# One v load cut in two, q tile 2 prepared earlier, and FFN steps regrouped in the opening of a fused attention and FFN kernel

## The chip, the cores and the metric

The kernel runs on one core of a Trainium2 chip. The metric is the device time of one execution in microseconds (us). The kernel before took 327.85 us (median of 3 runs, 327.48 to 328.96) when the prediction was made.

PE is the matmul engine, PEld its weight loads, DVE the vector engine, ACT the scalar engine, POOL the GpSimd engine, and SP the sync engine, which issues most loads. In the traces q1 is the queue of the loads that SP issues (hardware descriptors), and q0 the queue of the loads that POOL issues (software descriptors).

## The reference, cut to what matters

```python
# batch, heads, tokens, head_dim = 8, 8, 576, 64; d_model 512; d_ff 1536
r = np.maximum(x, 0.0)
phi(x) = np.concatenate([r * cos_w, r * sin_w], axis=-1)   # cos_w, sin_w by token
kv  = einsum('bhsf,bhsd->bhfd', phi(k), v);  z = sum(phi(k), axis=s)
x   = einsum(phi(q), kv) / (einsum(phi(q), z) + 1e-6)      # n/d below
xn  = x / rms(x) * rms_g
out = (silu(xn @ w_gate) * (xn @ w_val)) @ w_out
```

Everything before the FFN is small work for PE. The FFN is most of it: 12 steps of 128 columns for every 512 tokens, then the output matmuls.

## The kernel before

The kernel fills PE with FFN matmuls of one batch while DVE and ACT prepare the attention of the next. Only the opening, batch 0, has nothing to hide behind. It does, in this order: load k, q, v; phi of k; cast v to bf16; kvz, which is phi(k) times v with the sum z; copy kvz out of PSUM; n/d by tiles of 128 tokens; sum of squares (`x_sq`, ACT and POOL); normalize (`x_norm`, DVE); transpose x on PE; evacuate the transpose; FFN. `filler` matmuls keep PE busy meanwhile.

The parts that the change touches (cuts are marked):

```python
    load_kv("k", 0, *LOW); load_kv("k", 0, *HIGH)        # pairs of heads 0-1 and 2-3
    load_q_tokens(0, 0, 2)
    first_v = load_kv("v", 0, *LOW)
    load_kv("v", 0, 2, 3)
    load_kv("v", 0, 3, 4)                                # the last v pair, one DMA
    load_q_tokens(0, 2, 4)
    # ... constants, phi of k, q tiles 0 and 1, first v casts ...
    kvz_mm(0, low_banks, LOW)
    v_cast(V, 0, 3, 4, 0, 5)                             # V: DVE, A: ACT
    v_cast(A, 0, 3, 4, 5, NJ)
    kvz_copy(V, 0, 0, low_banks[0], LOW)
    kvz_copy(V, 0, 1, low_banks[1], LOW)
    kvz_mm(0, high_banks, (2, 3))
    # ... n/d of x tiles 0 and 1, x_sq, fillers, x_norm(0, 0) ...
    x_tr_pe(0, 0, psG[1][:, :])
    x_tr_evac(V, 0, 0, psG[1][:, :])
    q_tr_pe(0, 2, psO[0][:, :])
    q_tr_evac(A, 0, 2, psO[0][:, :])
    # ...
    open_ffn(0, (0,), 0, 128)                            # FFN step 0 for x tile 0
    x_tr_pe(0, 1, psV[1][:, :])
```

The FFN weights are loaded by POOL in ten slices, numbered 0 to 9, two for each range of columns. The load of k of batch 1 waits for slice 7. Its phi is put behind FFN steps 8 to 10, on DVE and ACT, in the same queues as the silu of those steps:

```python
    d = load_kv("k", 1)
    tc.add_manual_dep(d.ins, weight_dmas[7].ins.name, SYNC_DEP, reason="after the weights")
    gate_q = load_q(1)
    load_kv("v", 1, *LOW); load_kv("v", 1, *HIGH)
    # ...
    for j in range(NJ):
        at(0, 8 + j // 4, "post", k_phi, V, 1, j, 0)
        at(0, 8 + j // 4, "post", k_phi, A, 1, j, 1)
    for c in range(2):
        at(0, 10 + c, "post", q_phi, V, 1, c, 0)
        at(0, 10 + c, "post", q_phi, A, 1, c, 1)
    # ... later, among the output matmuls of batch 0: phi of q tiles 2 and 3 of batch 1,
    # then v_cast of batch 1, then kvz_pe(1, psA) ahead of the fourth
```

## Time and profile before

| | before, first profile |
|---|---|
| span | 326.24 us |
| PE busy | 98% of the span |
| first v landing | 10.28 us |
| n/d of the first half of x tile 0 | 12.89 us |
| transposes of x tile 0 | 17.10 us |
| first 128x512 FFN matmul (step 6) | 30.76 us |
| first phi of k of batch 1 on ACT | 35.77 us |
| kvz of batch 1 on PE | 44.70 us |

The page's chain of waits, followed back from the last instruction; the first line is by engine, the second by line of the kernel:

```profile
PE 90%; DMA 2%; DVE 2%; ACT 2%; issue 1%; SPq 0%; POOL 0%; ACTq 0%
PE psG L425 26%; PE psC L445 26%; PE psV L425 26%; PE psA L281 3%; DMA rv<-in_v_dram 2%; PE psA L309 2%; PE psG L445 1%; PE psG L561 1%; PE psO L561 1%; PE psV L561 1%; ACT kpm L208 1%; PE psC L826 1%; PE psV L253 1%; ACT sg L434 0%; PE psA L316 0%
```

Nine tenths of the chain are PE. Loads appear only as the v load at the start. The timeline of PE shows the opening. Its columns are start, duration, engine, line, operation, what is written and read, shapes, count, and in brackets the idle time before and what ended it:

```profile
12.89 0.30 PE L325 MATMUL psV<-kvzs,qpT 128*128 128x65 bf16 x4
...
17.10 0.40 PE L411 MATMUL psG<-ident,xn 128*128 128x128 bf16 x4 [0.89 <-DVE xn L386]
...
18.03 0.39 PE L561 MATMUL psG<-xnT,wg 128*128 128x128 bf16 x4
...
18.68 0.40 PE L411 MATMUL psV<-ident,xn 128*128 128x128 bf16 x4
...
23.68 0.40 PE L411 MATMUL psA<-ident,xn 128*128 128x128 bf16 x4
...
30.76 1.03 PE L425 MATMUL psG<-xnT,wg 128*128 128x512 bf16 x4
...
44.70 1.33 PE L281 MATMUL psA<-vvm,kpm 64*128 64x65 bf16 x72
```

The transposes of x tile 0 wait 0.89 us for the normalized x. From them to the first FFN matmul are 0.93 us, which the evacuation takes. From 30.76 us on, PE shows no idle time worth a mark.

### The profile page before, as it was taken

The page shows a single profiled execution, that of the slowest core. Times are in us where ns is not written, and L with a number is a line of the kernel's source. Part 1 is how long each engine was busy: PE and PEld are TensorE (multiplying, and loading weights), DVE is VectorE, ACT ScalarE, POOL GpSimd, SP SyncE. Part 2 cuts the span into 40 slices and gives each one's busy share as a digit, 9 for nine tenths or more (in the row PEclk, how much of TensorE's full clock was granted, in tenths as well). Part 3 has the DMA queues.
Part 4 walks back from the last instruction along what each step waited for, and adds up shares of the span by engine and source line. Part 5 has one row for each costly group of instructions (what it writes and reads, how often), then busy time and mean ns, then how long its engine had stood idle before and what let it go on. Part 6 is the DMA issues. An engine that isn't in the chain of part 4 may idle for free.

```text
span 326.2 us, 6439 instructions
## 1 busy us (share of the span) xinstructions
PE 318.8 (98%) x2442; PEld 161.0 (49%) x2442; DVE 186.3 (57%) x414; ACT 175.6 (54%) x364; POOL 32.3 (10%) x67
## 2 busy tenths in 40 slices
PE   8989999999999999999999999999999999999995
PEld 2478465554445444544454445444544444444443
DVE  6775668787755766578257745773577133203410
ACT  6774775865666457645655476556644233223321
POOL 1660212001100110010001100110011000000000
PEclk9999999999999999999999999999999999999999
DMA  7999999799969956976597569957621400020014
GB/s 254 247 186 238 353 196 343 276 172 211 264 181 159 236 166 178 204 210 173 170 223 204 156 187 229 188 161 218 123 44 32 131 32 0 27 104 1 0 34 96
DMA packets 80193, 53.91 MB, mean 165 GB/s; under 512 B 51361, under 2 KB 67489, under 8 KB 80162
## 3 DMA queue, kind: packets, MB, share of 16 engines
q1 hardware_dynamic: 73120, 48.64, 57.9%
q0 software_dynamic: 6880, 4.72, 10.0%
q8 instruction: 19, 0.31, 0.4%
q10 hardware_dynamic: 162, 0.13, 0.1%
q14 instruction: 12, 0.10, 0.1%
HBM read 37.75 MB, written 9.44 MB: 145 GB/s over the span
## 4 chain that ended last, share of the span: by engine, by line
PE 90%; DMA 2%; DVE 2%; ACT 2%; issue 1%; SPq 0%; POOL 0%; ACTq 0%
PE psG L425 26%; PE psC L445 26%; PE psV L425 26%; PE psA L281 3%; DMA rv<-in_v_dram 2%; PE psA L309 2%; PE psG L445 1%; PE psG L561 1%; PE psO L561 1%; PE psV L561 1%; ACT kpm L208 1%; PE psC L826 1%; PE psV L253 1%; ACT sg L434 0%; PE psA L316 0%
## 5 line engine op out<-in xcount | busy, mean ns | idle before, releaser
L440 DVE TENSOR_TENSOR hT<-psV,sg 128x512 bf16<-128x512 f32 x102 | 70.3, 689 | 96.6 <-PE psV L425 84.9
L434 ACT ACTIVATE sg<-psG 128x512 f32<-128x512 f32 x102 | 60.5, 594 | 64.9 <-PE psG L425 64.8
L425 PE MATMUL psG<-xnT,wg 128*128 128x512 bf16 (+1 forms) x368 | 92.9, 375 | 0.1
L425 PE MATMUL psV<-xnT,wv 128*128 128x512 bf16 (+1 forms) x368 | 92.7, 374 | 0.0
L445 PE MATMUL psC<-wo,hT 128*128 128x512 bf16 x396 | 89.6, 379 | 0.0
L425 PEld LDWEIGHTS <-wv 128*128 128x128 bf16 x416 | 40.6, 98 | 47.4
L445 PEld LDWEIGHTS <-hT 128*128 128x128 bf16 x420 | 40.2, 98 | 46.4
L425 PEld LDWEIGHTS <-wg 128*128 128x128 bf16 x416 | 38.6, 98 | 41.3 <-DVE xnT L264 0.4
L262 ACT COPY osb<-psC 128x512 f32<-128x512 f32 (+1 forms) x33 | 19.2, 582 | 40.7 <-PE psC L445 39.4
L379 POOL TENSOR_TENSOR rs<-ms,mhalf 128x1 f32<-128x1 f32 x36 | 20.0, 556 | 200.7 <-ACT scr L374 200.7
L374 ACT ACTIVATE scr<-xt 128x513 bf16<-128x513 f32 x36 | 22.9, 635 | 24.0 <-DVE xt L363 22.9
L386 DVE SCALAR_TENSOR_TENSOR xn<-xt,rs,gb 128x512 bf16<-128x512 f32 x36 | 26.8, 745 | 14.7 <-POOL rs L379 14.7
L208 ACT ACTIVATE kpm<-rk,tab 128x256 bf16<-128x256 f32 (+1 forms) x78 | 31.8, 477 | 1.6 <-DMA rk<-in_k_dram 1.6
L363 DVE TENSOR_TENSOR xt<-psA,rec 128x512 f32<-128x512 f32 x35 | 24.2, 691 | 1.2
L210 DVE TENSOR_SCALAR kpm<-rk,tab 128x256 bf16<-128x256 f32 (+1 forms) x84 | 22.1, 329 | 2.1 <-DMA rk<-in_k_dram 2.1
L208 ACT ACTIVATE qp<-rq,tab 128x512 bf16<-128x512 f32 x31 | 21.7, 712 | 0.0
L210 DVE TENSOR_SCALAR qp<-rq,tab 128x512 bf16<-128x512 f32 x33 | 15.5, 484 | 0.2 <-DMA rq<-in_q_dram 0.2
L309 PEld LDWEIGHTS <-qpT 128*128 128x128 bf16 x248 | 11.6, 98 | 6.7 <-issue 0.3
L309 PE MATMUL psA<-kvzs,qpT 128*128 128x65 bf16 x248 | 12.8, 194 | 0.2
L425 PE MATMUL psG<-xnt_tail,wg 128*128 128x512 bf16 x48 | 12.3, 379 | 0.0
L425 PE MATMUL psV<-xnt_tail,wv 128*128 128x512 bf16 x48 | 12.3, 379 | 0.0
L281 PEld LDWEIGHTS <-kpm 64*128 64x128 bf16 x576 | 9.9, 95 | 3.9 <-issue 2.9
(89 smaller groups left out, 168.4 us busy)
## 6 DMA issues: line engine op xcount, KB each, us to landing
out_dram<-osb SPq DMA_DIRECT2D x32, 256.0 KB, 2.9
rv<-in_v_dram SPq DMA_DIRECT2D x22, 288.0 KB, 3.4
rk<-in_k_dram SPq DMA_DIRECT2D x20, 288.0 KB, 3.6
rq<-in_q_dram SPq DMA_DIRECT2D x20, 256.0 KB, 3.2
rk<-in_k_dram SPq DMA_DIRECT2D x2, 1152.0 KB
rq<-in_q_dram SPq DMA_DIRECT2D x2, 1024.0 KB, 10.7
rv<-in_v_dram SPq DMA_DIRECT2D x3, 576.0 KB, 9.7
wo<-in_moe_w_out_dram POOLq DMA_DIRECT2D x4, 384.0 KB, 6.9
```

The lines of the kernel that those rows point to most:

```text
L208: nc.scalar.activation(out=out_ap, in_=in_ap, func=AF.Relu, scale=scale)
L210: eng.tensor_scalar(out=out_ap, in0=in_ap, scalar1=scale, scalar2=0.0, op0=ALU.mult, op1=ALU.max)
L281: nc.tensor.matmul(banks[c][:, r * E : (r + 1) * E], lhsT=kp_main[b][lo : lo + 64, j, r, :], rhs=vvm[b % 2][lo : lo + 64, r, j, :], start= ...
L309: nc.tensor.matmul(o[:, g, i, :], lhsT=qpT[(b, 0)][:, h, j * P : (j + 1) * P], rhs=kvz_of(b, h), start=True, stop=True,)
L363: nc.vector.tensor_tensor(out=xt[:, 0:DM].rearrange("p (b h d) -> p b h d", b=2, d=D), in0=o[:, :, :, 0:D], in1=rec[:, :, :].unsqueeze(3). ...
L374: nc.scalar.activation(out=scr[:, :], in_=xt[:, 0 : DM + 1], func=AF.Square, scale=1.0 / math.sqrt(DM), accum_out=ms[:, :],)
L379: nc.gpsimd.tensor_tensor(out=rs[:, :], in0=ms[:, :], in1=mhalf[:, :], op=ALU.pow)
L386: nc.vector.scalar_tensor_tensor(out=xn[:, :], in0=x_of[(b, j)][:, 0:DM], scalar=rs_of[(b, j)][:, :], in1=gb[:, :], op0=ALU.mult, op1=ALU. ...
L425: nc.tensor.matmul(pst[bank][:, cols[0] : cols[1]], lhsT=w[:, t, n * P : (n + 1) * P], rhs=x[:, t, cols[0] : cols[1]], start=(t == 0), sto ...
L434: nc.scalar.activation(out=sg[:, :], in_=psG[bank][:, :], func=AF.Silu)
L440: nc.vector.tensor_tensor(out=hTs[blk][:, n, :], in0=psV[bank][:, :], in1=sg[:, :], op=ALU.mult)
L445: nc.tensor.matmul(bank, lhsT=hTs[blk][:, n, j * P : (j + 1) * P], rhs=wo[:, n, :], start=(n == 0), stop=(n == NNT - 1),)
```

## The change

The intent was to shorten the opening: let the casts of the last v pair begin when its first piece has landed, free DVE of the low kvz copies, use ACT's and PE's idle time around 14 to 17 us for q tile 2, and give PE two FFN steps wherever it waited for the next x tile. The core of the diff:

```diff
-    def load_kv(which, b, r0=0, r1=4):
+    def load_kv(which, b, r0=0, r1=4, j0=0, j1=NJ):
... (source and target take columns j0 * D to j1 * D)
-    load_kv("v", 0, 3, 4)
+    load_kv("v", 0, 3, 4, 0, 5)
+    load_kv("v", 0, 3, 4, 5, NJ)
...
     kvz_mm(0, low_banks, LOW)
+    kvz_copy(A, 0, 0, low_banks[0], LOW)
+    kvz_copy(A, 0, 1, low_banks[1], LOW)
     v_cast(V, 0, 3, 4, 0, 5)
-    v_cast(A, 0, 3, 4, 5, NJ)
-    kvz_copy(V, 0, 0, low_banks[0], LOW)
-    kvz_copy(V, 0, 1, low_banks[1], LOW)
+    v_cast(V, 0, 3, 4, 5, NJ)
     kvz_mm(0, high_banks, (2, 3))
-    filler(1, idle)
-    kvz_mm(0, high_banks, (3, 4))
-    q_tr_evac(A, 0, 1, psO[0][:, :], (0, 4))
     nd_half(0, 0, 0, psV[0])
     nd_post_half(0, 0, 0, psV[0])
+    q_tr_evac(A, 0, 1, psO[0][:, :], (0, 4))
+    kvz_mm(0, high_banks, (3, 4))
     kvz_copy(A, 0, 0, high_banks[0], HIGH)
     kvz_copy(A, 0, 1, high_banks[1], HIGH)
+    filler(1, idle)
...
+    q_phi(A, 0, 2, 1)
     x_sq(0, 0)
...
+    q_phi(A, 0, 2, 0)
     x_sq(0, 1)
...
-    q_phi(A, 0, 2, 1)
-    filler(9, psV[1][:, :])
+    filler(7, psV[1][:, :])
+    q_tr_pe(0, 2, psO[0][:, :])
     x_norm(0, 0)
-    q_phi(V, 0, 2, 0)
+    q_tr_evac(A, 0, 2, psO[0][:, :])
     q_phi(A, 0, 3, 1)
+    filler(1, psV[1][:, :])
...
     x_tr_evac(V, 0, 0, psG[1][:, :])
-    q_tr_pe(0, 2, psO[0][:, :])
-    q_tr_evac(A, 0, 2, psO[0][:, :])
...
-    open_ffn(0, (0,), 0, 128)
+    open_ffn(0, (0, 1), 0, 128)
     x_tr_pe(0, 1, psV[1][:, :])
     x_tr_evac(V, 0, 1, psV[1][:, :])
-    open_ffn(0, (1,), 0, 128, first=1)
...
-    open_ffn(2, (4,), 0, 256, parts=(0,))
+    open_ffn(2, (4, 5), 0, 256, parts=(0,))
     x_tr_pe(0, 2, psA[:, 0, :])
     x_tr_evac(A, 0, 2, psA[:, 0, :])
-    open_ffn(2, (5,), 0, 256, first=1, parts=(0,))
```

More of the change, by code (lines that the diff above doesn't have):

```diff
@@ L79, in load_kv @@
         return nc.sync.dma_start(
-            out=raw[key][:, r0:r1, :],
+            out=raw[key][:, r0:r1, j0 * D : j1 * D],
             in_=src[b, 2 * r0 : 2 * r1, :, :]
             .rearrange("h s d -> (h s d)")
-            .rearrange("(r p n) -> p r n", p=P, n=NJ * D),
+            .rearrange("(r p n) -> p r n", p=P, n=NJ * D)[:, :, j0 * D : j1 * D],
         )
```

## The prediction

> **What bounds the kernel.** The page gives a span of 326.2 us with PE busy 98%, and the chain of waits puts 90% on PE. From about 31 us on PE runs without a gap over 0.4 us, and none there waits for a DMA (waits of PE and PEld after 30 us). The change touches only the opening, 10 to 25 us, so it can only move when that stream begins.
>
> **The opening, from the timeline and the chain.** DMA gates it until the last v pair lands near 11.8; then kvz of that pair 12.49 to 12.95; second n/d half; its xt on DVE at 14.37; x_sq on ACT 14.89; rs on POOL 15.69; xn on DVE 16.30 to 17.05; x transposes on PE at 17.10. Fillers cover PE to 16.2, then 0.89 us idle. After 17.10 I see three places where PE loses time: 0.7 us from the x transposes to the first FFN matmul (the evacuation; the eight q transposes, 0.44 us, hide inside it), 0.2 us before 18.68 (xn of x tile 1), 0.3 us before 23.68 (xn of x tile 2).
>
> **The change, costed.**
> 1. *v in two pieces, low copies to ACT.* One more issue (0.44 to 0.6 us on a queue that runs 6 us ahead of the data). The runs fall from 2304 to 1280 and 1024 bytes, above the 512 bytes that the Trainium skill ("DMA: Bandwidth & Descriptors", Specifications) gives for line rate; no run here has tested it. DVE now casts both pieces (0.49 and about 0.4 us), so the last kvz stays near 12.5. But ACT copies the low kvz at about 11.85 to 12.3 (DVE: 12.22 to 12.70), so n/d half 0 goes from 12.89 to about 12.35 and its DVE work (0.83 us) ends near 13.5 instead of 14.05. DVE was what held half 1 (PE finished it at 13.73, DVE began it at 13.97). Half 1, x_sq, rs, xn and the x transposes move forward 0.2 us, to about 16.9.
> 2. *q tile 2 ahead.* Phi moves from DVE (0.48) to ACT (0.71) and fits in ACT's idle time around 14 and between the x_sq; q lands at 13.3. Its transposes fill PE's idle time. They were in the shadow of the evacuation: worth about 0.
> 3. *Two FFN steps before x tile 1's transposes.* Removes the 0.2 us wait at 18.68. Gain 0.2.
> 4. *Steps 4 and 5 before x tile 2's transposes.* Removes 0.3 us at 23.68; its evacuation is still covered, by 0.87 us of matmuls, just enough.
>
> Sum about 0.7 us, all on the chain. Weights land at least 1 us before use (wv slice 0 at 17.1 for 18.1), as do q, v and wo of the next batch, so the stream should keep the shift to the end.
>
> **Prediction.** 327.2 us (before: 327.85), 8 in 10 between 326.4 and 328.1. Faster by over 2%: 0.01; within 2%: 0.98; slower by over 2%: 0.01.
>
> **What would show it.** The timeline: n/d half 0 before 12.5; x transposes of tile 0 near 16.9; no gap ahead of tile 1's transposes nor tile 2's; the first 128x512 FFN matmul of step 6 at about 30.1 instead of 30.76; the same distance from there to the end.
>
> **What would make it wrong.** The second v piece landing over 0.3 us later; phi of q tile 2 holding ACT when x_sq could start; the q transposes or the filler behind them holding the x transposes; DMA holding the later stages.

## More of the kernel before

Times are medians of 3 to 11 runs. Each set of runs was made on one chip, the later sets on four different ones, so times are compared only within a set or as ratios to the kernel before. All runs compared here were fast, that is within 1.5% of the fastest of their kernel.

The timeline of ACT around the next batch's k (the last line is the cast of v of batch 1):

```profile
35.28 0.60 ACT L434 ACTIVATE sg<-psG 128x512 f32<-128x512 f32 x1 [1.13 <-PE psG L425]
35.77 1.69 ACT L208 ACTIVATE kpm<-rk,tab 128x256 bf16<-128x256 f32 x4
...
43.25 1.15 ACT L262 CAST vvm<-rv 128x1152 bf16<-128x1152 f32 x1
```

The phi of k begins directly behind the silu of step 8 and shows no wait. From there to the v cast ACT is never idle, and the kvz of batch 1 on PE follows that cast.

## The result

Before 328.25 us (median of 6 runs, 327.48 to 329.6), changed 329.09 us (6 runs, 328.53 to 329.76). The ratio is 1.0023, with a 95% interval of 0.9998 to 1.0048. Ratios here are formed from the fast runs of both kernels in the same rounds, so they are not quite the ratio of the medians quoted. The two lie within 2% of each other, as forecast, but the time is above the forecast range and the forecast gain did not come.

The changed kernel's chain of waits, first profile (span 327.92 us; its line numbers are one higher than before, four higher for the opening's FFN matmuls):

```profile
PE 83%; DMA 8%; ACT 4%; DVE 1%; issue 1%; SPq 1%; POOL 0%; ACTq 0%
PE psC L446 26%; PE psG L426 24%; PE psV L426 24%; DMA rk<-in_k_dram 3%; PE psA L282 3%; DMA wv<-in_moe_w_val_dram 3%; DMA rv<-in_v_dram 2%; PE psA L310 2%; ACT kpm L209 2%; PE psG L446 1%; ACT sg L435 1%; PE psC L826 1%; PE psV L254 1%; ACT qp L209 0%; PE psA L317 0%
```

PE's share fell from 90% to 83%, and two loads are new: a weight slice (wv) and k of batch 1. The timeline of PE, at the same places as before:

```profile
12.74 0.37 PE L326 MATMUL psV<-kvzs,qpT 128*128 128x65 bf16 x4
...
17.47 0.40 PE L412 MATMUL psG<-ident,xn 128*128 128x128 bf16 x4
18.38 0.38 PE L565 MATMUL psG<-xnT,wg 128*128 128x128 bf16 x4 [0.52 <-DVE xnT L265]
...
19.27 0.39 PE L412 MATMUL psV<-ident,xn 128*128 128x128 bf16 x4
...
23.95 0.39 PE L412 MATMUL psA<-ident,xn 128*128 128x128 bf16 x4
...
30.59 1.03 PE L426 MATMUL psG<-xnT,wg 128*128 128x512 bf16 x4
...
39.64 1.02 PE L426 MATMUL psG<-xnT,wg 128*128 128x512 bf16 x4 [0.25 <-ACT sg L435]
...
43.20 0.38 PE L446 MATMUL psG<-wo,hT 128*128 128x512 bf16 x1 [1.03 <-ACT sg L435]
...
46.13 1.33 PE L282 MATMUL psA<-vvm,kpm 64*128 64x65 bf16 x72
```

Measured from the first v landing, which came at 10.84 us in this run and at 10.28 before, the opening became shorter: step 6 starts 19.75 us after it, and 20.48 before. That is the forecast gain, 0.73 us. But then PE waits twice for a silu, at 39.64 and at 43.20, and kvz of batch 1 is 1.43 us later than before instead of earlier. The timeline of ACT shows why:

```profile
35.11 0.60 ACT L435 ACTIVATE sg<-psG 128x512 f32<-128x512 f32 x1 [1.13 <-PE psG L426]
37.40 1.71 ACT L209 ACTIVATE kpm<-rk,tab 128x256 bf16<-128x256 f32 x4 [1.70 <-DMA rk<-in_k_dram]
39.01 0.57 ACT L435 ACTIVATE sg<-psG 128x512 f32<-128x512 f32 x1
...
44.89 1.15 ACT L263 CAST vvm<-rv 128x1152 bf16<-128x1152 f32 x1
```

ACT has done the silu of step 8 at 35.7 us and then stands for 1.70 us until k of batch 1 has landed. The silu of step 9, which PE needs, comes behind the phi of k in ACT's queue. The chain in order of time (start, duration, what), from 17 us on, says the same:

```profile
18.56 8.88 DMA wv<-in_moe_w_val_dram
...
27.46 9.91 DMA rk<-in_k_dram
...
37.40 0.03 ACT kpm L209
...
37.81 1.29 ACT kpm L209 x3
...
43.20 0.38 PE psG L446
...
46.20 1.27 PE psA L282 x72
```

A weight slice issued at 18.56 us lands at 27.4; that releases the load of k, which takes 9.91 us; then ACT works without a pause until its cast of v ends at 46.04, 0.09 us before PE's kvz.

The 1.68 us between the two profiled spans add up from six stretches: the first v landing +0.56, from it to the x transposes -0.19, from them to step 6 -0.54, from step 6 to the first phi of k +1.80, from that to kvz -0.20, and from kvz to the end +0.25.

### The profile page after: what moved, and what is told of

It reads as the page before. It is cut to its first block, busy times and chain, and to the rows that moved or that the text cites. A ratio compares the mean times of both kernels' runs of the same rounds, so it can differ in the third digit from the quotient of the medians.

```text
span 327.9 us, 6438 instructions
## 1 busy us (share of the span) xinstructions
PE 318.9 (97%) x2441; PEld 161.0 (49%) x2441; DVE 185.9 (57%) x412; ACT 176.5 (54%) x366; POOL 32.1 (10%) x67
## 4 chain that ended last, share of the span: by engine, by line
PE 83%; DMA 8%; ACT 4%; DVE 1%; issue 1%; SPq 1%; POOL 0%; ACTq 0%
PE psC L446 26%; PE psG L426 24%; PE psV L426 24%; DMA rk<-in_k_dram 3%; PE psA L282 3%; DMA wv<-in_moe_w_val_dram 3%; DMA rv<-in_v_dram 2%; PE psA L310 2%; ACT kpm L209 2%; PE psG L446 1%; ACT sg L435 1%; PE psC L826 1%; PE psV L254 1%; ACT qp L209 0%; PE psA L317 0%
## 5 line engine op out<-in xcount | busy, mean ns | idle before, releaser
L209 ACT ACTIVATE qp<-rq,tab 128x512 bf16<-128x512 f32 x32 | 22.5, 714 | 0.2 <-DMA rq<-in_q_dram 0.2
```

Source lines behind the costliest of these rows:

```text
L209: nc.scalar.activation(out=out_ap, in_=in_ap, func=AF.Relu, scale=scale)
```

## The experiments

There were two theories at the start. **K**: the gain of the opening is real, but the phi of k of batch 1 can't begin before k lands, and from there on ACT's queue, not PE, decides, so the time is k's landing plus a constant. **S**, the rival: cutting the v load delays the loads of the opening. A second rival, **O**, came with the second set: PE's own work in the opening decides, and k was late by chance in one profile only. Later a third matter, **T**, came up: the longer tail.

Each kernel was profiled once and timed against the kernel before. All the profiles, cut at the same five marks (us; "v" is the first v landing, "x" the transposes of x tile 0, "s6" the first 128x512 matmul, "phi" the first phi of k of batch 1 on ACT, "kvz" the first kvz of batch 1 on PE; the runs in the order of their sections):

| run | v | v to x | x to s6 | s6 to phi | phi to kvz | kvz to end | span |
|---|---|---|---|---|---|---|---|
| before | 10.28 | 6.82 | 13.66 | 5.01 | 8.93 | 281.54 | 326.24 |
| changed | 10.84 | 6.63 | 13.12 | 6.81 | 8.73 | 281.79 | 327.92 |
| before_again | 9.38 | 7.13 | 13.66 | 5.92 | 8.73 | 281.53 | 326.35 |
| after_again | 10.52 | 6.63 | 13.12 | 5.91 | 8.73 | 281.79 | 326.70 |
| no_split | 10.07 | 6.63 | 13.12 | 6.97 | 8.73 | 281.54 | 327.06 |
| after_k5 | 10.04 | 6.70 | 13.12 | 5.01 | 9.17 | 281.77 | 325.81 |
| before_k5 | 10.66 | 7.27 | 13.65 | 5.01 | 8.93 | 281.54 | 327.06 |
| after_k9 | 10.21 | 6.63 | 13.12 | 6.75 | 8.73 | 281.78 | 327.22 |
| before_k9 | 9.97 | 6.82 | 13.66 | 5.95 | 8.73 | 281.52 | 326.65 |
| after_q | 10.24 | 6.64 | 13.12 | 7.20 | 7.80 | 282.23 | 327.23 |
| after_k6 | 10.81 | 7.41 | 13.12 | 5.01 | 8.93 | 281.77 | 327.05 |
| before_k6 | 10.02 | 6.84 | 13.66 | 5.01 | 8.93 | 281.55 | 326.01 |
| part_front | 10.03 | 6.63 | 13.66 | 6.13 | 8.73 | 281.77 | 326.95 |
| part_ffn | 10.50 | 7.65 | 13.30 | 5.48 | 8.73 | 281.54 | 327.20 |
| split_only | 10.02 | 6.84 | 13.66 | 5.83 | 8.73 | 281.76 | 326.84 |
| no_split_k6 | 10.02 | 6.63 | 13.12 | 5.01 | 8.93 | 281.56 | 325.27 |
| no_split_k6_warm | 10.23 | 6.73 | 13.12 | 5.55 | 8.73 | 281.54 | 325.90 |

"x to s6" depends on the order of the FFN, and under the new order also on where the q transposes are (13.30 in part_ffn, 13.12 elsewhere). "s6 to phi" is 5.01 wherever the phi follows the silu of step 8, and more wherever ACT waited for k. "phi to kvz" is 8.73 whenever ACT waited, unless its queue was changed (after_q); kvz then begins 0.09 or 0.10 us after ACT's cast of v ends, and 0.30 us or more after it where ACT did not wait, so it is ACT's queue that PE follows. "kvz to end" has only two values but for after_q. The times:

| run | median us | kernel before, same rounds | ratio | 95% interval |
|---|---|---|---|---|
| after_again | 328.60 | 328.45 | 1.0007 | 0.9986 to 1.0027 |
| before_again | 328.38 | 328.45 | 1.0002 | 0.9988 to 1.0016 |
| no_split | 328.86 | 328.45 | 1.0010 | 0.9996 to 1.0024 |
| after_k5 | 328.08 | 328.45 | 0.9989 | 0.9974 to 1.0004 |
| after_k9 | 329.71 | 328.50 | 1.0035 | 1.0009 to 1.0061 |
| before_k9 | 328.93 | 328.50 | 1.0021 | 0.9997 to 1.0045 |
| before_k5 | 328.86 | 328.50 | 1.0002 | 0.9981 to 1.0023 |
| after_q | 328.31 | 328.50 | 0.9991 | 0.9968 to 1.0014 |
| after_k6 | 328.32 | 328.87 | 0.9991 | 0.9973 to 1.0009 |
| before_k6 | 328.07 | 328.87 | 0.9989 | 0.9969 to 1.0010 |
| part_front | 328.66 | 328.87 | 1.0003 | 0.9983 to 1.0023 |
| part_ffn | 328.87 | 328.87 | 1.0002 | 0.9979 to 1.0025 |
| split_only | 328.44 | 328.84 | 0.9985 | 0.9970 to 1.0001 |
| no_split_k6 | 327.57 | 328.84 | 0.9966 | 0.9949 to 0.9982 |
| no_split_k6_warm | 327.59 | 328.84 | 0.9961 | 0.9949 to 0.9974 |

All of these are within 2%, and most of the intervals include 1. Apart from after_k9 and the last two, the verdicts below therefore rest on the profiles and not on the times.

### after_again and before_again: the two kernels once more

No edit. 

> The changed kernel once more. The question is whether the two profiles differ by the change or by chance. Theory K (the load of k of batch 1 decides): the opening is about 0.7 us shorter in each profile relative to the landing of the first v pair, and the scalar engine's first phi of k of batch 1 starts when that k lands, not when its silu is done; the time is k's landing plus a constant. If the late weights of the first profile (131 KB per us instead of 190 from 13 to 18 us) were chance, k lands near 35.8 here and the span is near 326.2; if the change causes them, k lands at 37 again and the span is near 327.9.

> The kernel before once more, as a measure of chance. Theory K: the phi of k of batch 1 starts at the landing of k or right after the silu of step 8 at 35.8, whichever is later; span 326 to 327.5 with k's landing moving from run to run by up to 1 us. Time ratio to before 1.000 within 0.003.

The changed kernel's opening repeated to 0.01 us. k landed at 36.16, near the earlier of the two values expected, but the phi still waited for it; the span was 326.70, not the 326.2 expected. The kernel before brought the surprise. Its timeline of ACT and its chain:

```profile
34.69 0.60 ACT L434 ACTIVATE sg<-psG 128x512 f32<-128x512 f32 x1 [1.13 <-PE psG L425]
36.09 1.70 ACT L208 ACTIVATE kpm<-rk,tab 128x256 bf16<-128x256 f32 x4 [0.81 <-DMA rk<-in_k_dram]
```

```profile
PE 82%; DMA 7%; DVE 4%; ACT 3%; issue 1%; POOL 0%; ACTq 0%; DVEq 0%
PE psC L445 26%; PE psG L425 24%; PE psV L425 24%; DMA rk<-in_k_dram 4%; DMA wv<-in_moe_w_val_dram 3%; PE psA L281 3%; PE psA L309 2%; ACT kpm L208 2%; PE psG L445 1%; DVE kpm L210 1%; ACT sg L434 1%; PE psC L826 1%; PE psV L253 1%; DVE vvm L264 1%; DVE qp L210 1%
```

In this profile the kernel before waits for k as well: the phi starts 0.81 us late, PE waits 0.56 us for a silu, and k's load and a weight slice are in the chain with PE at 82%. The first profile of before, in which nothing waited, was the lucky one. (Its 7.13 us from v to x is no slow clock: v landed at 9.38 us, and DVE was busy until it could begin the cast at 9.72.) The slow stretch of weights in the first profile of the changed kernel (143 and 91 GB/s in 15:16 and 16:17 us, against 182 and 188 before) also comes without the change: before_again shows 142 and 120 GB/s in 14:15 and 15:16.

### no_split: the changed kernel with one v load

```diff
-    load_kv("v", 0, 3, 4, 0, 5)
-    load_kv("v", 0, 3, 4, 5, NJ)
+    load_kv("v", 0, 3, 4)
```

> The changed kernel with the last v pair loaded in one DMA again. Rival S (the split itself delays the DMA of the opening): v lands at 10.3 instead of 10.84, weights stream at 190 KB per us, k lands near 35.8, time about 1 us under the changed kernel, 327.5 to 328. Theory K without S: landing times and time as the changed kernel within 0.5 us.

v landed at 10.07, but k was no earlier and the time no better (328.86), so S as the cause of the late k falls. The opening is as short without the split (6.63 and 13.12) as with it. The split gains nothing. The first v landing ranges from 9.38 to 10.66 us over the nine profiles without the split and from 10.02 to 10.84 over the eight with it; the ranges overlap, so no delay of the loads is shown. The row holds one more difference: the tail is 281.54 here and 281.79 in the changed kernel.

### after_k5 and before_k5: k of batch 1 issued earlier, in both kernels

```diff
-    tc.add_manual_dep(d.ins, weight_dmas[7].ins.name, ...)
+    tc.add_manual_dep(d.ins, weight_dmas[5].ins.name, ...)
```

> The changed kernel with the load of k of batch 1 gated on weight slice 5 instead of 7, so issued about 4 us earlier. Theory K: k lands before 34.5, the scalar engine no longer waits for it, and the gain of the opening shows: 327.3 to 327.6 us against 328.25 before, 1.5 us under the changed kernel. If the hardware queue's load moves only once the weight queue has drained, k lands no earlier and the time stays near 329.

> The kernel before with k gated on weight slice 5, so early. Theory K: k no longer decides; the start of the step with 128x512 matmuls does, 20.5 us or more after the first v pair landed, and kvz 13.9 to 14.2 us after that. 328.2 to 328.5 us, that is 0.5 to 0.8 us slower than the changed kernel with the same gate was. Rival: no difference from the changed kernel with the early gate, 328.1 or less; then the opening's gain is not worth anything even without the wait.

In the changed kernel k landed at 32.27 us, and ACT no longer waited for it (timeline of ACT):

```profile
34.38 0.60 ACT L435 ACTIVATE sg<-psG 128x512 f32<-128x512 f32 x1 [1.13 <-PE psG L426]
34.87 1.69 ACT L209 ACTIVATE kpm<-rk,tab 128x256 bf16<-128x256 f32 x4
```

Its span, 325.81, is lower than both of the changed kernel's. In time it gained less than expected (328.08, not 327.3 to 327.6). Part of this is that k and the last weight slices are now under way together: slice 9, issued at 19.29, landed at 36.09, where in the changed kernel it was issued at 20.03 and landed at 31.27. The chain in order of time shows that this is just too late for PE:

```profile
19.29 16.79 DMA wv<-in_moe_w_val_dram
36.09 0.05 issue
36.13 1.04 PE psV L426 x4
```

before_k5 also lost its wait for k. Its profile fell into a run with a slow clock (below), so its 7.27 must not be set against 6.63. Its time, 328.86, is above the 328.2 to 328.5 expected; three of its six runs had the low mean clock (0.994) of such a run. The 0.78 us between the medians of the two kernels lie in different rounds on different chips; they go the way that K says, but do not show it.

### after_k9 and before_k9: k of batch 1 issued later, in both kernels

```diff
-    tc.add_manual_dep(d.ins, weight_dmas[7].ins.name, ...)
+    tc.add_manual_dep(d.ins, weight_dmas[9].ins.name, ...)
```

> The changed kernel with the load of k of batch 1 gated on weight slice 9 instead of 7, so later. Theory K (from the landing of that k on, the scalar engine's queue decides, and the PE's first kvz of batch 1 comes 8.7 us after its first phi): first phi near 38.7, kvz near 47.4, span near 329.2, measured time near 331, whatever the opening gained. Rival O (the opening's PE work decides, and k only happened to be late in one profile): time rises by under 0.5 us.

> The kernel before with the same late gate. Theory K: first phi near 38.5, time within 0.4 us of the changed kernel with the late gate, the opening's 0.7 us being invisible. Rival O: 0.7 us slower than the changed kernel with the late gate, or 1 us faster if the change itself costs time.

The size was a miss. k, issued some 4 us later than with slice 7, landed at 36.69 instead of the 38.7 expected. That is 26.48 us after the first v, no later than with slice 7 (26.3 to 27.0 in most profiles), so the spans did not rise. A load issued while weight slices are in flight sent its first packet 3.6 us later, this one, issued behind them, 1.0 us later (last section); and from that packet to its landing it took 4.65 us, where the two profiles of the changed kernel have 6.29 and 5.41. Once more phi to kvz was 8.73 in both, and the opening's difference was gone by the first phi, 26.50 and 26.43 us after v. The medians were 0.8 us apart, not within 0.4 as expected; 0.25 of it is the tail, and the ranges of the two (328.36 to 330.70 and 328.43 to 330.39) cover each other. The ratio of 1.0035 is not told apart from the changed kernel's own 1.0023 (0.9998 to 1.0048).

So this pair, meant to decide between K and O, does not. The earlier gates do. With gate 7 or 9 ACT waited for k in ten of eleven profiles, so k was not late by chance in one; with gate 5 or 6 the wait is gone in five of six, and "s6 to phi" is back at 5.01. O falls. That the gate moves the time is shown by no_split and no_split_k6 (below), which differ by the gate alone: 1.0010 of before (0.9996 to 1.0024) with slice 7, and, in other rounds, 0.9966 (0.9949 to 0.9982) with slice 6.

### after_q: ACT's and DVE's queues relieved behind k

```diff
-        at(0, 10 + c, "post", q_phi, V, 1, c, 0)
-        at(0, 10 + c, "post", q_phi, A, 1, c, 1)
+        at(0, 11, "post", q_phi, V, 1, c, 0)
+        at(0, 11, "post", q_phi, A, 1, c, 1)
... (v_cast of batch 1 ahead of phi of q tiles 2 and 3; q transposes of batch 1 one step later)
```

> The changed kernel with the scalar and vector queues relieved after the landing of k: phi of q of batch 1 moved behind the last silu, the casts of v of batch 1 ahead of half of those phi, the q transposes one step later. Theory K: kvz of batch 1 comes about 7.6 to 8.2 us after the first phi instead of 8.7, the wait of PE for the silu of step 11 shrinks from 0.5 us and over to under 0.2, and the time falls to 327.6 to 328.0. If it stays at 328.6, the scalar queue behind k is not what holds PE.

```profile
37.20 1.70 ACT L209 ACTIVATE kpm<-rk,tab 128x256 bf16<-128x256 f32 x4 [2.08 <-DMA rk<-in_k_dram]
...
43.46 1.15 ACT L263 CAST vvm<-rv 128x1152 bf16<-128x1152 f32 x1
```

The timeline of ACT shows the v cast at 43.46, 6.26 us behind the first phi, where it was 7.49 in the changed kernel. kvz came 7.80 us after the phi instead of 8.73, and 0.39 us after the end of that cast, no longer directly behind it. So it is the queue behind k that lies between k and kvz; the edit relieved ACT and DVE together, and their shares are not separated. PE's wait for the silu of step 11 was 0.42 us, where the changed kernel had 1.03, but not under the 0.2 expected. Half of the gain came back later: the tail was 0.44 us longer than in the changed kernel. I did not follow where. k was 2.08 us late in this profile, and the time (328.31, not the 327.6 to 328.0 expected; ratio 0.9991) is not told apart from before.

### after_k6 and before_k6: the gate between

```diff
-    tc.add_manual_dep(d.ins, weight_dmas[7].ins.name, ...)
+    tc.add_manual_dep(d.ins, weight_dmas[6].ins.name, ...)
```

> The changed kernel with k of batch 1 gated on weight slice 6, between the 5 and the 7 tried. Theory K: k lands near 34 and no longer holds the scalar engine, and the last weight slice lands before 35.5, so PE does not wait for it as it did at 36.09 with gate 5. First phi of k 5.0 us after the first 128x512 matmul, kvz 13.9 us after that matmul; ratio to before 0.997 to 0.999, span near 325.7. If k still lands after 35.5, no gain over gate 7.

> The kernel before with the same gate. Theory K: k was at most just late in it, so ratio to before 0.999 to 1.001, and 0.5 to 0.9 us slower than the changed kernel with gate 6.

With slice 6 neither kernel waits for k or for a weight slice: 5.01 and 8.93 in both rows. before_k6 was a little better than expected (328.07), and the changed kernel was not faster than it in time. Its profile explains part of this: after_k6 ran with a slow clock in the opening and lost 0.78 us there (7.41 instead of 6.63). The runs of both scatter by over 1 us, and this pair alone settles nothing.

The slow clock shows in the stretches view (stretch and its length in us; busy us of PE, PEld, DVE, ACT and POOL with counts; then granted PE clock, DMA share and GB/s). Here 9.0 to 12.5 us of part_ffn, and below it the same of the first profile of before:

```profile
9.00:12.50 3.50, 3.50 (x36) 2.36 (x37) 3.15 (x6) 2.97 (x7) 1.70 (x3) 0.52 0.92 295
```

```profile
9.00:12.50 3.50, 3.21 (x76) 2.11 (x75) 3.09 (x8) 3.00 (x6) 1.92 (x3) 1.00 0.93 285
```

Three of the 17 profiles (before_k5, after_k6, part_ffn) ran at half clock for some 3.4 us here. In the 50 runs of the kernel before in the later sets (before_again's among them), 9 had a mean granted clock of 0.995 or less, about what such a stretch leaves in the mean; they took 329.09 us on average, the other 41 took 328.52. This chance, 0.57 us, is nearly as large as the gain that is being looked for. (Such runs still count as fast.)

### part_front and part_ffn: each half of the change alone

part_front is the changed kernel with the FFN order of before; part_ffn is the kernel before with only the regrouped FFN steps:

```diff
-    open_ffn(0, (0,), 0, 128)
+    open_ffn(0, (0, 1), 0, 128)
     x_tr_pe(0, 1, psV[1][:, :])
     x_tr_evac(V, 0, 1, psV[1][:, :])
-    open_ffn(0, (1,), 0, 128, first=1)
... (the same for steps 4 and 5 around x tile 2)
```

> The changed kernel with the FFN order of before, so only the front: v pieces, copies, phi and transposes of q tile 2. From the first v landing to the x transposes 6.65 us (before 6.8 to 7.3, changed 6.63), from there to the first 128x512 matmul 13.65 as before, not 13.1; time not told apart from before, since k decides.

> The kernel before with only the FFN order of the change. From the first v landing to the x transposes 6.8 to 7.3 us as before, from there to the first 128x512 matmul 13.1 to 13.2 instead of 13.66; time not told apart from before, since k decides.

The front is worth 0.19 us (6.63 against 6.82) and nothing after the x transposes (13.66). (part_ffn's own 7.65 is the slow clock's, above the 6.8 to 7.3 expected.) The FFN order alone is worth 0.36 (13.30), less than expected; with the q transposes out of the way it is worth the whole 0.54 (13.12). In part_ffn the trace has n/d of x tile 2 starting at 20.35 us on PE, released at 20.30 by ACT's evacuation of those q transposes, after 0.16 us in which PE loaded no weights; in the changed kernel it waits for nothing. So the q transposes moved ahead are worth nothing alone and 0.18 us together with the regrouped steps. Which part of the front brings the 0.19 was not separated further; no_split excludes the split of the load, which leaves the copies on ACT and the reordered n/d. In both profiles k decided in the end, and neither time differs from before.

### split_only: the kernel before with the last v pair in two loads

```diff
-    load_kv("v", 0, 3, 4)
+    load_kv("v", 0, 3, 4, 0, 5)
+    load_kv("v", 0, 3, 4, 5, NJ)
```

> The kernel before with only the last v pair in two pieces, its casts as before. Theory T (one more DMA turns the order in which the sync engine checks landings at the end): from the first kvz of batch 1 to the end 281.78 us, as in every kernel with the split, instead of 281.53; the opening as before (first v landing to x transposes 6.8 us or more), k deciding; time 0.0 to 0.5 us over before. Rival: the tail stays 281.53, then the longer tail comes from another part of the change.

The tail was 281.76, so the split alone does it. In all seven profiles with the split and the original later stages it is 281.76 to 281.79 (after_q is left aside), in all nine without it 281.52 to 281.56. The trace shows where. At the end SP waits for the semaphores of the DMAs one after the other, about 0.06 us each. In the kernel before the first such wait ends 280.20 us after kvz, at the landing of SP's last store, and the last store of ACT, which lands at 280.44, is only looked for some waits later. In the changed kernel the first wait ends at 280.45, and seven more follow. The issue view of the last two stores (KB, and us from issue to landing; the landing that the trace lacks is the one with no number), of before and of the changed kernel:

```profile
out_dram<-osb SPq DMA_DIRECT2D x1, 32.0 KB
out_dram<-osb ACTq DMA_DIRECT2D x1, 32.0 KB, 2.0
```

```profile
out_dram<-osb SPq DMA_DIRECT2D x1, 32.0 KB, 1.8
out_dram<-osb ACTq DMA_DIRECT2D x1, 32.0 KB
```

The stores were issued at the same distance from kvz in both (278.39 us). The landing recorded for ACT's store in before, 2.0 us after its issue, fits the first wait's end in the changed kernel. One more DMA at the start turned the order in which the semaphores are used, and the latest one came first. The semaphore numbers in the traces bear this out: the first wait is for number 100 in both, which tells of SP's last store in before and of ACT's in the changed kernel, while ACT's store in before has number 118, the one looked for last. It is so in all 17 profiles: ACT's last store has number 100 in the eight with the split and 118 in the nine without. How the numbers are given out was not looked into; that the split brings the 0.25 us is shown. The time of split_only (0.9985, up to 1.0001) does not show it: 0.25 us is less than the scatter.

### no_split_k6 and no_split_k6_warm: both losses taken away

no_split_k6 is the changed kernel with one load for the last v pair and k of batch 1 gated on slice 6; the second has `filler(2, idle)` in place of `filler(1, idle)` behind each paced matmul of the opening, against the slow clock.

> The changed kernel without the split and with k of batch 1 gated on weight slice 6: both things that hid the opening's gain taken away. Theory K with T: at full clock, first v landing to first 128x512 matmul 19.75, then 13.93 to kvz, then 281.53: span 315.2 us after the first v landing, 325.3 where that lands at 10.1; the kernel before, held by k, has 316.8 (26.5 + 8.73 + 281.53). Ratio to before 0.995 to 0.998. If under 0.1 us faster than before, the accounting is wrong.

> The same with two fillers behind each paced matmul of the opening instead of one. In three of 14 profiles the granted clock of PE halved from about 9.5 to 12.5 us, and the x transposes came 0.5 to 0.8 us later after the first v landing. If idle PE time before that is the reason, no dip here and less scatter: lowest times as without it, highest 0.5 us lower. If the clock dips for another reason, no difference.

The chain of waits and the timeline of ACT of no_split_k6:

```profile
PE 91%; ACT 4%; DVE 2%; issue 1%; DMA 1%; ACTq 0%
PE psC L445 26%; PE psG L425 26%; PE psV L425 26%; PE psA L281 3%; PE psA L309 2%; ACT kpm L208 2%; PE psG L445 2%; PE psG L564 1%; DMA rk<-in_k_dram 1%; PE psV L564 1%; PE psO L564 1%; PE psC L825 1%; PE psV L253 1%; ACT qp L208 1%; ACT sg L434 0%
```

```profile
34.29 0.60 ACT L434 ACTIVATE sg<-psG 128x512 f32<-128x512 f32 x1 [1.13 <-PE psG L425]
34.78 1.69 ACT L208 ACTIVATE kpm<-rk,tab 128x256 bf16<-128x256 f32 x4
```

PE is back at 91% of the chain, and the phi follows the silu. The span is 325.27 with the first v landing at 10.02. That is the best pair, since before_k6 had its v at 10.02 as well, the same full clock in the opening and no wait for k: 326.01. The difference, 0.74 us, is the opening's gain (20.50 - 19.75 = 0.75 us from v to step 6), now whole at the end of the kernel. It is one pair of profiles, from different chips. In time the version takes 0.9966 of before (interval 0.9949 to 0.9982), 1.3 us by the medians. That is below the 2% at which the class changes, but clear of noise, and clear of the changed kernel's ratio (1.0023, from 0.9998), which comes from other rounds. It keeps the change without the split and adds the earlier gate, so not all of it is the change's: before_k6, with the gate alone, has 0.9989 (0.9969 to 1.0010). These intervals overlap, so in time the change's own share is not shown.

The warm version is as fast (0.9961). Neither it nor no_split_k6 had a slow-clock run among six, so whether the extra fillers help is not settled. Its profile had k late by 0.54 us again: gate 6 makes the wait rare, not impossible.

## Why the prediction was wrong, point by point

- *What bounds the kernel: "none there waits for a DMA".* True of the one profile it was read from, not of the kernel. In the second profile of before, PE waits 0.56 us behind ACT, which waits for k. In the first, the phi of k started directly behind a silu with no wait, so k had landed, but nothing in that view says by how much. I took "no wait" for "room". The trace does allow an estimate: q of batch 1, issued right behind k, landed at 38.59 us, and in the five profiles with gate 7 that give both landings q comes 2.9 us (2.89 to 2.95) after k. So k landed near 35.7 in that profile, only some 0.1 us before its phi began at 35.77.
- *Front, gain 0.2.* Right in size: 6.82 to 6.63. The reason given, that DVE was freed early by the copies on ACT, fits, but was not tested apart from the new order of n/d; the v split was not needed for it, as no_split shows. In the changed profile n/d half 0 came 1.90 us after the first v landing instead of 2.61. The Trainium skill ("DMA: Bandwidth & Descriptors", Specifications) asks for 512 bytes or more for line rate, and the pieces of 1280 and 1024 bytes agree with that to within some 0.1 us: with the split the last v landed 1.55 to 1.69 us after the first, without it 1.52 to 1.57.
- *q tile 2, gain 0.* Right alone (part_front 13.66), and it was needed for the next term.
- *FFN order, gain 0.2 + 0.3.* Right: 0.54 for all of it.
- *"Weights land at least 1 us before use [...], as do q, v and wo of the next batch, so the stream should keep the shift to the end."* This is the step that failed. The list leaves out k of batch 1. I had looked at the landings of q, v and wo; for k the trace gave none, and I went on. k needs to land by 5.01 us after step 6 starts, its load is started by the weights and not by PE (slice 7 releases it, and the first slice waits for the first v load), and it lands about 26.5 us after the first v landing whatever PE's opening does (26.3 to 27.0 in nine of the ten profiles in which it decided at gate 7 or 9, 25.66 in after_again, and 25.40 at gate 6 in the warm version). The kernel before wants it 20.48 + 5.01 = 25.49 us after v, the changed one 19.75 + 5.01 = 24.76. So the shorter opening only makes a longer wait for the same load. The first profile of before, which the prediction was read from, escaped by luck: there phi came 25.50 us after v. Term by term: the hand-over from step 6 to phi was put at no change, and was 0.9 and 1.8 us longer than 5.01 in the two profiles of the changed kernel.
- *The tail.* Not foreseen at all: 0.25 us from one more DMA.
- *The time.* Gain 0.73 in the opening, of which nothing reached the end, and 0.25 lost. The measured medians are +0.84 us in the first set and +0.15 in the second, both with intervals that include no change. The sum of the known terms is near +0.25; the rest is not told apart from the scatter of k's landing and of the clock.

Among the dangers that the prediction named, "DMA holding the later stages" was the true one. The slow clock is not among them, and its effect was nearly as large as the gain.

## What to carry to other kernels

Before moving work forward, look for the next load that this work will meet and that does not move along: find its landing, its gate and its first reader, and take a missing landing as an open question. An instruction that starts exactly when its predecessor ends tells nothing about how long its data had been there, so profile twice before calling a stretch free of waits. An in-order queue turns one late load into late work for everyone behind it: here the silu that PE needed stood behind the phi of k.

## What the Trainium skill lacked or had wrong

- "DMA: Bandwidth & Descriptors", Specifications, gives about 0.6 us to the first byte for loads from the sync queue, and its section on queues says that an engine takes turns between the queues that have work. Here, counted from the start of the issuing instruction (which itself takes about 0.5 us), the first packet of q1 came 1.1 us after the first issue of the kernel, but 3.47 to 3.77 us after the issue of k of batch 1 in each of the fifteen profiles with gates 5 to 7, where weight slices of q0 were still outstanding. It came after 1.05 and 1.02 us in the two with gate 9, where all ten slices had landed and q0 had only the end of a load of w_out left. The DMA view of before from 27.5 to 30 us, with k issued at 26.99, has q0 only, at 204 GB/s:

```profile
DMA packets 638, 0.51 MB, mean 204 GB/s; under 512 B 21, under 2 KB 638, under 8 KB 638
q0 software_dynamic: 638, 0.51, 129.5%
```

  From 30.5 to 33 us q1 has most of it, and the rate is 341 GB/s:

```profile
DMA packets 458, 0.85 MB, mean 341 GB/s; under 512 B 11, under 2 KB 150, under 8 KB 458
q1 hardware_dynamic: 308, 0.71, 75.5%
q0 software_dynamic: 150, 0.14, 33.8%
```

  No page that I read has such a delay. Its mechanism is open.
- "TensorE: Matmul & The Clock Gate", Part 1 and "Why this matters for your kernels", lets the clock fall to half after an idle window of about 3.4 us and advises no idle gap over about 3 us. In the three profiles with the half clock no gap of PE after its first instruction at 1.2 us was longer than 0.94 us, and before_k6 with a gap of 1.67 us kept its clock. Part 1 also says that short idle times, when frequent enough, can make the clock swing, but gives no size for them; here PE was busy for 72 to 78% of the 3.41 us before the three falls, while before_k6 had such a stretch at 51% and no fall. So the runs do not show what set it off. How long it lasted, 3.4 us or so, agrees with the page's window.
- No page that I read says that the end of a program looks at its DMA semaphores one by one (about 0.06 us each here), nor that one DMA more at the start can lengthen the end by 0.25 us.
